# The result's turn runs ahead of the scores in their block, states are turned six steps behind their load, and the opening's pieces get other ranks

## The chip, the cores and the metric

One core of a Trainium2 chip runs the whole program. The metric is the device time of one execution in microseconds (us); of several runs the median is taken. Engines go by the names of the profile: PE is TensorE (matrix products, and transposes as products with an identity), PEld its weight loads, DVE is VectorE, ACT is ScalarE, SP issues the transfers (DMA).

## The reference, cut to what matters

```python
# x: B=8, H=8, S=512, D=64; state: B, H, Ns=32, D
scale = 1 / sqrt(D)
a      = softmax(scale * x @ state.T)          # [B,H,S,Ns]
xread  = a @ state                             # [B,H,S,D]
a2     = softmax(scale * state @ x.T)          # [B,H,Ns,S]
sread  = a2 @ x                                # [B,H,Ns,D]
attn   = concatenate([xread, sread], axis=2)   # [B,H,S+Ns,D]
x2     = attn.transpose(0, 2, 1, 3).reshape(4352, 512)
h      = x2 @ w_in                             # w_in: 512 x 2048
g      = h * clip(h + 3, 0, 6) / 6             # hardswish
out    = g @ w_out                             # w_out: 2048 x 512
```

All inputs and the output are float32.

## The kernel before, in words

**Numbers.** Float32 products at full precision are made of three fast products: each operand is split into a high part (ACT, L246) and a low part (DVE, L247), and hi·hi, hi·lo and lo·hi are added up in one bank (`product`, L831). Only the first batch's first quarter of the hidden width uses plain float32 matmuls (L860 for the first product, L900 for the second), since its split operands are not there yet.

**Steps.** The hidden width of 2048 has 16 pieces of 128. A step is one batch (512 tokens) with one such piece, or one piece for the 256 state tokens at the end; there are 144. `first(n)` (L836) makes h into a bank `ps_h` (L831, or L860); ACT (L881) and DVE (L883) make g of it; L246 and L247 split g; `second(n)` (L890) multiplies with the rows of w_out (L831, or L900) into the four accumulators `acc`. The second product of a step comes two steps behind its first. The order of the steps is: batch 0 quarter 0, batch 1 quarter 0, batch 0 quarter 1, batch 1 quarter 1, then the later quarters of batch 0, those of batch 1, batches 2 to 7 whole, and the state tokens.

**Tokens' side.** The read of the states by tokens is folded into the weights: W' is state times w_in by heads (matmuls L458 in 64x32 tiles of the array), so that the first product is the softmax weights `aT` times W'. The scores of a batch are L458 as well, w_in's place being taken by x turned (`xT`), and `stT` being the state turned. Where W' of batch 0 is made for the first quarter, its columns come in three pieces of 128, 128 and 256; the row with 256 columns is called the second half in what follows.

**State's side.** `scores_by_columns` (L654) is one block on PE: the 16 score matmuls of batch b, then, from batch 2 on, two riders of the batch before: a transpose (L791) of the result of the batch before that one (the tile `tmp` `sr`, which DVE's L805 makes) and the 64 small matmuls of the read (L796), both into one bank `ps_h`. DVE copies the turned result into `sread_t` (L770), the input of the state tokens' steps. `tokens_read_alone` runs the same for the last batch, with no scores.

**States.** `load_state` (L368) lets SP load the state of a batch into `st_raw`, a tile with one buffer (L382 from batch 2 on, 4 transfers of 32x4x32 in a row of the order), and DVE turn it into `stT` (L389). The scores of the batch, and its W', read `stT`.

**Order.** Every piece of work is told to a planner (class `Plan`) with its engine, a cost, a rank, the keys it reads and writes, and pieces that it must stand behind. The planner holds a modelled clock for PE, DVE, ACT and SP; each time it takes, among the pieces that can start nearly first on an engine, the one of lowest rank (the number may be negative), and so fixes a serial order for each of the four. A rank is about the number of the step in which the piece is wanted. Some tiles have few buffers, which the planner holds too: `raw` 3, `ot` 2, `tmp` 10, `ps_h` 2, `ps_s` 2, one each of `xb` and `st_raw`. Up to the first step of the program, planned gaps of PE are filled with transposes of the identity into `ps_h` (L1127), which compute nothing.

**The opening's lines.** x of batch 0 is scored by rows on PE; DVE ends that softmax with L582. L630 turns the softmax weights back (8 transposes). L546 turns x of batch 1, in two halves of 8 transposes, by way of two `ps_s` banks that ACT copies out. L316, L320 and L327 are DVE's passes that clamp and round a weight (into `w_in`, `raw` or `early`); L303 loads weights. L693 and its neighbours are the softmax of batch 0's late scores (L458 out of `xT`), which only the state's side needs, and whose small transposes are L731. L354 is a low part of w_out made from a `raw` tile. L445 loads x turned into `raw` for batch 2, and L752 moves the blocks of the read weights from one `tmp` tile to another, 32 small transfers for batch 1. L674 turns scores on DVE.

**Where ranks stand.** `weights` (L987) has a row for each early piece of w_in and w_out; its last two numbers are the ranks of the passes on DVE and of the load. `LATE` and `LATE_STEP` do the same for the late pieces of w_in, and `HALVES` for a piece split in halves. `fetch` (L1058) tells the loads of a later batch: the state of batch b with step s0, which is 7 steps ahead of the step in which its scores are told.

Of the kernel before, what the change touches and what calls it, by code (L numbers as in the profile page):

```python
# [10 lines left out]
F32 = mybir.dt.float32  # L11
# [138 lines left out]
def tile_state_attention_then_hardswish_ffn(  # L150
# [8 lines left out]
    nc = tc.nc  # L159
# [209 lines left out]
    def load_state(b, rank, after=()):  # L369
        key = ("st_raw", b)  # L370

        def load():
            raw = get(key, lambda: att.tile([P, NG, D], F32, name="st_raw", bufs=1))
            for u in range(NG):
                nc.sync.dma_start(raw[:, u, :], st_v[b, :, :, u, :])

        def load_blocks():
            raw = get(key, lambda: att.tile([P, NG * D], F32, name="st_raw", bufs=1))
            for u in range(NG):
                for k in range(D // NS):  # L380
# [8 lines left out]
        V(0.22, rank + 1.0, lambda: nc.vector.transpose(  # L389
            get(("stT", b), lambda: att.tile([P, P], F32, name="stT")), made[key]), [key], [("stT", b)])  # L390

    def x_key(b):
        return ("ot", "x1") if b == 1 else ("xb", b)
# [258 lines left out]
    def scores_by_columns(b, rank, after=(), name="C"):  # L652

        ps = [("ps_s", (name, b, u)) for u in range(NG)]  # L654
        riders = [tokens_read(b - 1, "ps_h")] if b >= TURNED or name == "L" and b else []

        def run():
            all_heads(b, [bank(k) for k in ps], lambda q: xT(b, q))
            for _, read, _, _, _ in riders:
                read()  # L660

        T(1.22 + sum(r[0] for r in riders), rank, run,
          [("stT", b)] + [xT_key(b, q) for q in range(NQ)] + [k for r in riders for k in r[2]],
          ps + [k for r in riders for k in r[3]], after)
        for r in riders:
            r[4]()
        return ps
# [107 lines left out]
    def tokens_read(b, tag="ps_s"):  # L775
# [11 lines left out]
        last_key = [("tmp", ("sr", c)) for c in last]  # L787

        def read():
            for key in last_key:  # L790
                nc.tensor.transpose(bank(pr)[:, place(1)], tmp(key)[:, : NG * D], ident)  # L791
            for u in range(NG):
                for j in range(J):
                    for q in range(NQ):
# [9 lines left out]
        def then():  # L804
# [3 lines left out]
                [pr, ("r2", (b, 0))], [sr_key])  # L808
            for c in last:
                put(c, pr, place(1))  # L810
        return 1.0 + 0.11 * len(last), read, [*t_key, *x_parts, *last_key], [pr], then

    def tokens_read_alone(b, rank, after=()):
        cost, read, reads, writes, then = tokens_read(b)
        T(cost + 0.2, rank, read, reads, writes, after)
        then()

    def result_turned(b, rank, after=()):
# [156 lines left out]
    for seg, (b, c0, c1) in enumerate(segments):  # L975
# [8 lines left out]
    seen = set()  # L984

    weights = [
        (0, "in", 0, 1, ("early0", 0, 0), -5.67, -19.58), (1, "in", 1, 1, ("early0", 0, 1), -3.50, -8.04),  # L987
        (2, "in", 2, 2, ("early1", 0), 0.77, -7.20), (-0.34, "out", 0, 1, ("raw", ("out", 0)), -2.50, -6.17),
        (-0.90, "out", 1, 1, ("raw", ("out", 1)), -0.36, -1.02), (0.55, "out", 2, 1, ("raw", ("out", 2)), 2.49, -3.00),
        (5.05, "out", 3, 1, ("early3", 0, 0), 2.13, -1.44),  # L990
    ]
# [3 lines left out]
    PLACES = {  # L995
# [68 lines left out]
    at(6, lambda: [f(4.88 + 0.2 * k) for k, f in enumerate(late_halves)])  # L1064
    at(9, halves_of_first, 9.5)
    for b, s0 in (0, 4), (1, 8):

# [24 lines left out]
    load_x(0, -14.96)  # L1092
    weights_until(0.7)
    load_state(1, -4.23)
    accs = [f"acc{q}" for q in range(NQ)]
    take_in(0, -14.82, (), accs)
    tokens_by_rows(0, lambda k: -2.51, lambda k: (), accs)
    load_x(1, -3.76)
    for n in range(len(steps)):
        tell(n)  # L1100
# [6 lines left out]
        elif b < 2 and n % FPC == 0:  # L1107
            ends = wp_parts[b, c][1:] + [FPC]
            for f0, f1 in zip(wp_parts[b, c], ends):
                weights_until(n + f1 - 1)  # L1110
                s = n - 3 + f0
                wprime(b, [(c, f0, f1)], s + 0.41 if n else (11.83, -6.49, 0.01)[f0],
                       ["acc2", "acc3"] if n == 0 and f1 < 3 else None,
                       [first_of[s]] if n >= 8 else ())
        if n == 0:
            take_in(1, -0.41, [scores_at[0]])
            rank1 = lambda k: (1.71, 2.50, 1.58, -2.06, 0.41)[k]
            tokens_by_columns(1, rank1, scores_by_columns(1, 1.99, [wp_at[0, 0, 2]]))
        for f, a in events.get(n, ()):
            f(*a)  # L1120
        first(n)
# [36 lines left out]
```

## Time and profile before

| | us |
|---|---|
| runs of before (3) | 663.09 to 663.54 |
| median | 663.51 |
| the profiled execution | 663.73 |
| its span (first to last instruction) | 661.9 |
| around the span | 1.8 |
| busy: PE, DVE, ACT | 651.0, 420.2, 310.8 |
| PE's three-part second products, L831 into `acc` | 3 x 528 matmuls, 209.1 + 205.6 + 205.9 |
| PE's first products, L831 into `ps_h` with split weights of a batch | 3 x 248, 90.7 + 89.7 + 89.7 |
| scores and W', L458 | 384 matmuls, 24.0 |

Busy times of matmuls overlap, since each is counted from its issue to its modelled end; what one costs in a row of them is the distance between two starts. The page divides the span into 40 slices; the busy share of PE in tenths is 8 in the second slice, 0 in the first, 7 in the last and 9 in all others. The clock that PE was granted is 9 (90% or more) in every slice. The transfers move 46.26 MB in all, and their engines are busy 9, 8, 0 and 7 tenths in the first four slices, and less behind.

How the lines are read: in the timeline and in the list of PE's rows a line has the start in us, the time from its start to the end of its last instruction, the engine, the line of the kernel, the operation, the tile written and the tiles read, then for PE the tile of the array (128*128 is all of it), the shape and the type, and how many instructions it groups; in brackets stands the idle time before it, and the instruction that ended it. In the list of groups the number behind the count is the time busy, then the mean of one in ns, then the idle time before. Tiles of one name are told apart by buffer numbers in the order's rows and not in the trace's.

### The profile page before, as it was taken

Reading aid. Unit: us, or ns where it says so; the run is one execution under the profiler, and the core shown is the slowest. Engines: PE = TensorE matmul, PEld = TensorE weight load, DVE = VectorE, ACT = ScalarE, POOL = GpSimd, SP = SyncE. Lnnn points to the kernel's source line nnn. Section 1 sums busy time; section 2 is a strip of 40 time slices with the busy share of each in tenths; the row PEclk is TensorE's granted clock in tenths of the full one; section 3 lists DMA queues with packets and bytes.
Section 4 is the critical chain, followed back from the end, with each engine's and each line's share of the span. In section 5 each row is a group of like instructions: output and inputs, shape, how many; then the busy total and the mean of one; then the engine's idle time right before and its main releaser. Section 6 shows DMA issues by size and latency. Waiting matters only on the chain.

```text
span 661.9 us, 9937 instructions
## 1 busy us (share of the span) xinstructions
PE 651.0 (98%) x3950; PEld 502.5 (76%) x3950; DVE 420.2 (63%) x697; ACT 310.8 (47%) x520; POOL 1.0 (0%) x7
## 2 busy tenths in 40 slices
PE   8899999999999999999999999999999999999997
PEld 7446777777686877787877877787778788788896
DVE  4998999885846945953677356944585353543542
ACT  5888777543523543443444343633343343333542
POOL 0000000000000000000000000000000000000000
PEclk9999999999999999999999999999999999999999
DMA  9807452415052243314050503132131001000101
GB/s 272 308 0 214 133 181 81 96 27 139 13 109 74 34 70 94 66 26 70 1 132 9 84 5 109 24 52 44 65 65 24 8 1 65 1 0 1 64 0 33
DMA packets 130894, 46.26 MB, mean 70 GB/s; under 512 B 119200, under 2 KB 121248, under 8 KB 130720
## 3 DMA queue, kind: packets, MB, share of 16 engines
q1 hardware_dynamic: 130704, 45.37, 27.9%
q8 instruction: 31, 0.51, 0.3%
q10 hardware_dynamic: 144, 0.26, 0.1%
q14 instruction: 15, 0.12, 0.1%
HBM read 33.03 MB, written 8.91 MB: 63 GB/s over the span
## 4 chain that ended last, share of the span: by engine, by line
PE 92%; DVE 3%; SPq 2%; DMA 2%; issue 0%; ACT 0%; DVEq 0%; ACTq 0%
PE acc L831 53%; PE ps_h L831 28%; PE ps_s L458 4%; PE acc L900 2%; DMA st_raw<-in_state_dram 2%; PE ps_h L458 2%; SPq L752 2%; PE ps_h L796 1%; PE ps_h L860 1%; PE ps_s L611 1%; SPq L382 0%; DVE g L883 0%; PE acc L546 0%; DVE g_lo L247 0%; DVE s L571 0%
## 5 line engine op out<-in xcount | busy, mean ns | idle before, releaser
L831 PE MATMUL acc<-w_out_hi,g_hi 128*128 128x512 f32 x528 | 209.1, 396 | 0.0
L831 PE MATMUL acc<-w_out_hi,g_lo 128*128 128x512 f32 x528 | 205.6, 389 | 0.3 <-DVE g_lo L247 0.3
L831 PE MATMUL acc<-w_out_lo,g_hi 128*128 128x512 f32 x528 | 205.9, 390 | 0.0
L881 ACT ACTIVATE g<-ps_h,three 128x512 f32<-128x512 f32 (+1 forms) x144 | 95.6, 664 | 212.5 <-PE ps_h L831 208.2
L883 DVE SCALAR_TENSOR_TENSOR g<-g,ps_h 128x512 f32<-128x512 f32 (+1 forms) x144 | 94.5, 657 | 136.9 <-ACT g L881 136.2
L831 PEld LDWEIGHTS acc<-w_out_hi,g_hi 128*128 128x128 f32 x528 | 99.1, 188 | 35.5 <-issue 13.4
L246 ACT CAST g_hi<-g 128x512 fp32r<-128x512 f32 (+1 forms) x140 | 83.3, 595 | 85.1 <-DVE g L883 84.8
L247 DVE TENSOR_TENSOR g_lo<-g,g_hi 128x512 fp32r<-128x512 f32 (+1 forms) x140 | 92.0, 657 | 46.2 <-ACT g_hi L246 43.8
L831 PEld LDWEIGHTS acc<-w_out_hi,g_lo 128*128 128x128 f32 x528 | 99.1, 188 | 21.8 <-DVE g_lo L247 0.8
L831 PEld LDWEIGHTS acc<-w_out_lo,g_hi 128*128 128x128 f32 x528 | 99.2, 188 | 18.9
L831 PE MATMUL ps_h<-aT_hi,wp_hi 128*128 128x512 f32 (+1 forms) x248 | 90.7, 366 | 0.0
L831 PE MATMUL ps_h<-aT_hi,wp_lo 128*128 128x512 f32 (+1 forms) x248 | 89.7, 362 | 0.0
L831 PE MATMUL ps_h<-aT_lo,wp_hi 128*128 128x512 f32 (+1 forms) x248 | 89.7, 362 | 0.0
L831 PEld LDWEIGHTS ps_h<-aT_hi,wp_hi 128*128 128x128 f32 x248 | 46.8, 189 | 8.5 <-DVE wp_lo L247 0.3
L831 PEld LDWEIGHTS ps_h<-aT_lo,wp_hi 128*128 128x128 f32 x248 | 46.8, 189 | 8.2 <-DVE early L316 0.3
L831 PEld LDWEIGHTS ps_h<-aT_hi,wp_lo 128*128 128x128 f32 x248 | 46.8, 189 | 7.3
L831 PE MATMUL ps_h<-aT_hi,wp 128*128 128x512 f32 x128 | 44.6, 389 | 0.0
L831 PEld LDWEIGHTS ps_h<-aT_hi,wp 128*128 128x128 f32 x128 | 24.0, 188 | 5.0
L831 PE MATMUL ps_h<-aT_lo,wp 128*128 128x512 f32 x64 | 24.9, 389 | 0.0
L458 PE MATMUL ps_s<-w_in,stT 64*32 64x512 f32 (+1 forms) x384 | 24.0, 557 | 0.0
L537 DVE STREAM_TRANSPOSE tmp<-raw 128x512 f32<-128x512 f32 x24 | 16.4, 699 | 6.5 <-DMA raw<-in_x_dram 6.5
L247 DVE TENSOR_TENSOR wp_lo<-ps_s,wp_hi 128x512 fp32r<-128x512 f32 (+1 forms) x34 | 19.8, 621 | 0.3 <-ACT wp_hi L246 0.3
(119 smaller groups left out, 506.4 us busy)
## 6 DMA issues: line engine op xcount, KB each, us to landing
out_dram<-ot SPq DMA_DIRECT2D x8, 1024.0 KB, 4.5
early<-in_moe_w_in_dram SPq DMA_DIRECT2D x7, 1024.0 KB, 7.1
xb<-in_x_dram SPq DMA_DIRECT2D x28, 256.0 KB, 4.1
raw<-in_x_dram SPq DMA_DIRECT2D x96, 64.0 KB, 2.1
early<-in_moe_w_out_dram SPq DMA_DIRECT2D x4, 1024.0 KB, 5.5
raw<-in_moe_w_out_dram SPq DMA_DIRECT2D x7, 512.0 KB, 4.4
raw<-raw SPq DMA_DIRECT2D x96, 32.0 KB, 2.0
early<-in_moe_w_in_dram SPq DMA_DIRECT2D x2, 512.0 KB, 5.3
```

The lines of the kernel that those rows point to most:

```text
L246: S_(cost, rank, lambda: nc.scalar.copy(hi(), src()), reads, [writes[0]])
L247: V(cost, rank, lambda: nc.vector.tensor_tensor(lo(), src(), hi().bitcast(F32), op=ALU.subtract), [*reads, writes[0]], [writes[1]])
L458: nc.tensor.matmul(out[u][cols, :], made["stT", b][rows, cols], moving(q)[rows], start=True, stop=True,)
L537: V(0.7, rank, lambda q=q, key=key: nc.vector.transpose(xT(b, q), made[key][:, q % 2]), [(*key, q % 2, u, k) for u in range(2) for k in ra ...
L611: nc.tensor.matmul(out[:, j, q], xT(b, q)[:, js], apart[:, q], start=True, stop=True,)
L752: nc.sync.dma_start(dst[:, :, q], src[:, :, c])
L796: nc.tensor.matmul(bank(pr)[cols, u * D : (u + 1) * D], e2T(b, u)[:, j * P + q * NS : j * P + (q + 1) * NS], x_tile(b, True)[:, NG * q + u ...
L831: nc.tensor.matmul(ps, l, r, start=start and k == 0, stop=stop and k == n - 1)
L860: nc.tensor.matmul(bank(ps), made["wp_32", (b, k)][:, g, fs], a_first(g), start=g == 0, stop=g == NG - 1)
L881: S_(cost + 0.05, rank, lambda: nc.scalar.activation(g(), bank(ps)[:, :width], AF.Relu, bias=three), [ps], [g_key])
L883: V(cost, rank, lambda: nc.vector.scalar_tensor_tensor(g(), g(), 6.0, bank(ps)[:, :width], op0=ALU.min, op1=ALU.mult), [ps], [g_key])
L900: nc.tensor.matmul(bank(acc), made["g_hi", n][:, js], plain_out[i][1](), start=opens, stop=closes)
```

## The change

There are three edits.

The transposing of a result on PE is taken out of `read` in `tokens_read` and handed back as a function of its own, `first`, which `scores_by_columns` calls ahead of the scores; `tokens_read_alone` calls it directly ahead of the read, as it did.

DVE's turn of a state is taken out of `load_state`. A new function, `turn_state`, tells it, six steps behind the load, with a rank that is five higher than the one it had.

Ranks of the opening's pieces of weights, x, W' and softmax are replaced by others.

```diff
@@ load_state
         plan.add("Q", 1.8, rank, load_blocks, (), [key], after, 400.0)
-        V(0.22, rank + 1.0, lambda: nc.vector.transpose(
-            get(("stT", b), lambda: att.tile([P, P], F32, name="stT")), made[key]), [key], [("stT", b)])
+
+    def turn_state(b, rank, after):
+
+        key = ("st_raw", b)
+        V(0.22, rank, lambda: nc.vector.transpose(
+            get(("stT", b), lambda: att.tile([P, P], F32, name="stT")), made[key]), [key], [("stT", b)], after)
@@ scores_by_columns
         def run():
+            for r in riders:
+                r[5]()
             all_heads(b, [bank(k) for k in ps], lambda q: xT(b, q))
-            for _, read, _, _, _ in riders:
-                read()
+            for r in riders:
+                r[1]()
@@ tokens_read
         def read():
-            for key in last_key:
-                nc.tensor.transpose(bank(pr)[:, place(1)], tmp(key)[:, : NG * D], ident)
             for u in range(NG):
...
-        return 1.0 + 0.11 * len(last), read, [*t_key, *x_parts, *last_key], [pr], then
+
+        def first():
+            for key in last_key:
+                nc.tensor.transpose(bank(pr)[:, place(1)], tmp(key)[:, : NG * D], ident)
+        return 1.0 + 0.11 * len(last), read, [*t_key, *x_parts, *last_key], [pr], then, first
@@ weights and ranks
-        (0, "in", 0, 1, ("early0", 0, 0), -5.67, -19.58), (1, "in", 1, 1, ("early0", 0, 1), -3.50, -8.04),
...
+        (0, "in", 0, 1, ("early0", 0, 0), -22.54, -44.86), (1, "in", 1, 1, ("early0", 0, 1), -24.76, -19.99),
...
-    LATE, LATE_STEP, HALVES = (2.35, 6.00), (0.38, 0.50), 1.45
+    LATE, LATE_STEP, HALVES = (28.48, 9.19), (-14.22, -0.40), -9.26
@@ fetch
         at(s0 + 1, lambda: load_state(b, s0, [first_of[s0]]))
+        at(s0 + 7, lambda: turn_state(b, s0 + 6, [first_of[s0 + 6]]))
```

What the ranks do is read from the order. **PE, the opening**: the rows from the end of batch 1's first half of turned x to the first L900 of batch 0 (`acc`). `ident,ot` are turns of x, `ident,tmp` turns of softmax weights, `w_in,stT` pieces of W', `xT,stT` batch 0's late scores, `w_in,wp` the plain first product. Before:

```order
L1127 MATMUL ps_h<-ident 128x128 x5
L630 MATMUL acc_316<-ident,tmp 128x128 x4
L630 MATMUL acc_324<-ident,tmp 128x128 x4
L546 MATMUL ps_s<-ident,ot 128x128 x8
L860 MATMUL ps_h<-w_in_322,wp_243 128x512 x4
L458 MATMUL ps_s<-w_in_187,stT 32x256 x8
L900 MATMUL acc_382<-raw,g 128x512
```

After:

```order
L1140 MATMUL ps_h<-ident 128x128 x2
L550 MATMUL ps_s<-ident,ot 128x128 x8
L634 MATMUL acc_326<-ident,tmp 128x128 x4
L634 MATMUL acc_332<-ident,tmp 128x128 x4
L462 MATMUL ps_s<-xT,stT 32x512 x8
L872 MATMUL ps_h<-w_in_338,wp_243 128x512 x4
L737 MATMUL ps_s<-ident,tmp 128x128 x8
L912 MATMUL acc_394<-raw,g 128x512
L912 MATMUL acc_399<-raw,g 128x512
L912 MATMUL acc_404<-raw,g 128x512
L462 MATMUL ps_s<-w_in_160,stT 32x256 x8
```

Three of five fillers are gone; the second half of the turns stands ahead of the softmax weights' turns; batch 0's late scores stand ahead of the first product and their small transposes (L737 in the new lines, L731 before) behind it; the piece of W' with 256 columns stands behind three second products instead of ahead of the first. (A plain float32 matmul of the order is two instructions of the trace: x4 of `w_in,wp` here is x8 there, x8 of `xT,stT` is x16. Transposes count once.) Some 340 rows later, from step 28 on, PE's order is the old one but for the second edit.

**DVE, the opening**: from the end of the first softmax (L582 before, L586 after) to the w_in row that the piece with 256 columns reads (`w_in_187` before, `w_in_160` after). Before:

```order
L582 TENSOR_TENSOR tmp<-tmp,s_263 128x512 x2
L320 SCALAR_TENSOR_TENSOR raw<-raw 128x512
L327 SCALAR_TENSOR_TENSOR raw<-raw 128x512
L316 TENSOR_SCALAR early_106<-early_106 128x1024
L320 SCALAR_TENSOR_TENSOR early_106<-early_106 128x1024
L327 SCALAR_TENSOR_TENSOR w_in_187<-early_106 128x4x256
```

After:

```order
L316 TENSOR_SCALAR early_106<-early_106 128x1024
L699 TENSOR_REDUCE nm_354<-ps_s 128x1
L701 TENSOR_SCALAR nm_354<-nm_354 128x1
L699 TENSOR_REDUCE nm_362<-ps_s 128x1
L701 TENSOR_SCALAR nm_362<-nm_362 128x1
L316 TENSOR_SCALAR raw<-raw 128x512
L320 SCALAR_TENSOR_TENSOR raw<-raw 128x512
L706 TENSOR_SCALAR r_365<-r_365 128x2
L708 RECIPROCAL r_365<-r_365 128x2
L895 SCALAR_TENSOR_TENSOR g<-g,ps_h 128x512
L327 SCALAR_TENSOR_TENSOR raw<-raw 128x512
L320 SCALAR_TENSOR_TENSOR early_106<-early_106 128x1024
L327 SCALAR_TENSOR_TENSOR w_in_160<-early_106 128x4x256
```

The three rows ahead of those of after are the old ones. Between the clamp of `early` and its rounding now stand the softmax of batch 0's late scores (L699 to L708), three passes over `raw` and the first g (L895).

**PE, a block of scores** (here that of batch 3's scores, with the read of batch 2 and batch 1's result): the rows from the last first product to the next second product. Before:

```order
L831 MATMUL ps_h<-aT_hi,wp_lo 128x512
L458 MATMUL ps_s<-tmp,stT 32x512 x8
L791 MATMUL ps_h<-ident,tmp 128x128
L796 MATMUL ps_h<-xb,raw 32x64 x32
L831 MATMUL acc_1859<-w_out_hi_718,g_hi 128x512
```

After:

```order
L843 MATMUL ps_h<-aT_hi,wp_lo 128x512
L818 MATMUL ps_h<-ident,tmp 128x128
L462 MATMUL ps_s<-tmp,stT 32x512 x8
L800 MATMUL ps_h<-xb,raw 32x64 x32
L843 MATMUL acc_1856<-w_out_hi_738,g_hi 128x512
```

The transpose has changed places with the scores; the rest of the block stands as it did. This is so in six blocks.

**DVE, a state's turn** (that of batch 3, during step 28; `st_raw` has one buffer, and L674 turns the scores of batch 2 whose softmax follows). Before:

```order
L805 TENSOR_TENSOR tmp<-ps_h,r_752 128x128
L770 COPY sread_t<-ps_h 128x128
L674 STREAM_TRANSPOSE tmp<-ps_s 128x512 x2
L389 STREAM_TRANSPOSE stT<-st_raw 128x128
L247 TENSOR_TENSOR g_lo<-g,g_hi 128x512
L565 TENSOR_REDUCE m_1597<-tmp 128x16
```

After:

```order
L247 TENSOR_TENSOR wp_lo<-ps_h,wp_hi 128x512 x2
L247 TENSOR_TENSOR wp<-ps_s,wp 128x512 x2
L247 TENSOR_TENSOR aT_lo<-tmp,aT_hi 128x512
L764 STREAM_TRANSPOSE raw<-tmp 128x512
L895 SCALAR_TENSOR_TENSOR g<-g,ps_h 128x512
L764 STREAM_TRANSPOSE raw<-tmp 128x512
L895 SCALAR_TENSOR_TENSOR g<-g,ps_h 128x512
L247 TENSOR_TENSOR g_lo<-g,g_hi 128x512 x2
L393 STREAM_TRANSPOSE stT<-st_raw 128x128
```

The turn stands some 30 rows later, behind the softmax of batch 2 and not ahead of it. On SP the four loads of that state now stand ahead of the store of an output tile (`out_dram<-ot`, 128x2048) and not behind it.

More of the change, by code (lines that the diff above doesn't have):

```diff
@@ L810, in then, with run @@
                 put(c, pr, place(1))
-        return 1.0 + 0.11 * len(last), read, [*t_key, *x_parts, *last_key], [pr], then
+        def first():
+            for key in last_key:
+                nc.tensor.transpose(bank(pr)[:, place(1)], tmp(key)[:, : NG * D], ident)
+        return 1.0 + 0.11 * len(last), read, [*t_key, *x_parts, *last_key], [pr], then, first
     def tokens_read_alone(b, rank, after=()):
-        cost, read, reads, writes, then = tokens_read(b)
-        T(cost + 0.2, rank, read, reads, writes, after)
+        cost, read, reads, writes, then, turn_last = tokens_read(b)
+        def run():
+            turn_last()
+            read()
+        T(cost + 0.2, rank, run, reads, writes, after)
         then()
@@ L986, in tile_state_attention_then_hardswish_ffn @@
     weights = [
[L987 to L990 removed]
+        (0, "in", 0, 1, ("early0", 0, 0), -22.54, -44.86), (1, "in", 1, 1, ("early0", 0, 1), -24.76, -19.99),
+        (2, "in", 2, 2, ("early1", 0), 6.93, -9.11), (-12.37, "out", 0, 1, ("raw", ("out", 0)), -6.07, -6.01),
+        (-19.24, "out", 1, 1, ("raw", ("out", 1)), 1.25, 3.51), (-3.21, "out", 2, 1, ("raw", ("out", 2)), 0.76, 2.18),
+        (-1.73, "out", 3, 1, ("early3", 0, 0), 3.93, 1.24),
     ]
@@ L1111, in tile_state_attention_then_hardswish_ffn @@
                 s = n - 3 + f0
-                wprime(b, [(c, f0, f1)], s + 0.41 if n else (11.83, -6.49, 0.01)[f0],
+                wprime(b, [(c, f0, f1)], s + -0.92 if n else (39.35, -26.67, -5.60)[f0],
                        ["acc2", "acc3"] if n == 0 and f1 < 3 else None,
```

16 lines of the change are left out of this document (8 added, 8 removed).

## The prediction

> **What bounds the kernel now.** I read the page's busy line and the chain that ended last first, then the timeline of TensorE (PE) for every pause, then who ended each pause.
>
> ```profile
> span 661.9 us, 9937 instructions
> PE 651.0 (98%) x3950; PEld 502.5 (76%) x3950; DVE 420.2 (63%) x697; ACT 310.8 (47%) x520; POOL 1.0 (0%) x7
> PE 92%; DVE 3%; SPq 2%; DMA 2%; issue 0%; ACT 0%; DVEq 0%; ACTq 0%
> 20.28:29.00 8.72, 6.87 (x48) 3.78 (x46) 8.48 (x14) 7.59 (x17) 0.00 (x0) 1.00 0.99 369
> 29.00:111.30 82.30, 82.30 (x501) 53.23 (x502) 77.28 (x120) 64.55 (x100) 0.00 (x0) 1.00 0.43 134
> ```
>
> PE makes 92% of the chain. So the change can only gain in three places: where PE waits, where PE runs filler, and where it pays for changing shape. The last two rows are stretches (length, then PE, weight load, DVE, ACT). From 29.00 to 111.30 us PE has no pause, but DVE is busy 77.28 of 82.30 us: a second limit lies close behind. I look at the three places in turn.
>
> **1. The opening.**
>
> ```profile
> 20.28 0.71 PE L1127 MATMUL ps_h<-ident 128*128 128x128 f32 x5
> 21.55 1.26 PE L630 MATMUL acc<-ident,tmp 128*128 128x128 f32 x8 [0.56 <-DVE tmp L582]
> 22.64 1.04 PE L546 MATMUL ps_s<-ident,ot 128*128 128x128 f32 x8
> 23.51 3.60 PE L860 MATMUL ps_h<-w_in,wp 128*128 128x512 f32 x8
> 27.04 0.66 PE L458 MATMUL ps_s<-w_in,stT 64*32 64x256 f32 x16
> 29.00 1.17 PE L900 MATMUL acc<-raw,g 128*128 128x512 f32 x2 [1.29 <-DVE g L883]
> 36.94 1.09 PE L458 MATMUL ps_s<-xT,stT 64*32 64x512 f32 x16
> 37.96 1.98 PE L860 MATMUL ps_h<-w_in,wp 128*128 128x512 f32 x4
> ```
>
> Dead time of PE before: 0.71 of filler (L1127) and 0.56 of waiting before L630, 1.29 before the first L900; 2.56 us in all. After 29.00 PE runs through.
>
> By the changed order, the second half of batch 1's turns (L546 x8) and batch 0's scores (the L458 of 36.94, which holds PE 1.02 us, 36.94 to 37.96, and about 0.09 to enter) stand ahead of the first L860. I walk it with the rows' durations. The turns run from about 20.7 to 21.65, held by ScalarE's copies out of the two ps_s banks. L630 follows to 22.6, the scores to 23.7. The first L860 needs ScalarE's copies of L630, which now stand behind the two copies of the turns and end near 23.55, where they ended 23.49 before. So L860 starts at 23.7 instead of 23.51, with 1.11 us of scores already done. Its eight instructions end at 27.2, the state weights' turns (eight at 0.11) at 28.05. There the wait for the first g (1.29 before) should be over: VectorE's g now ends near 28.0.
>
> What is late next is the second half of batch 0's first W' (the L458 of 27.04), since its w_in columns come later on VectorE:
>
> ```profile
> 20.80 1.29 DVE L582 TENSOR_TENSOR tmp<-tmp,s 128x512 f32<-128x512 f32 x2
> 23.34 0.69 DVE L316 TENSOR_SCALAR early<-early 128x1024 f32<-128x1024 f32 x1
> 25.33 1.23 DVE L327 SCALAR_TENSOR_TENSOR w_in<-early 128x1024 uint32<-128x1024 uint32 x1
> 27.65 0.69 DVE L327 SCALAR_TENSOR_TENSOR raw<-raw 128x512 uint32<-128x512 uint32 x1
> L693 DVE TENSOR_REDUCE nm<-ps_s 128x1 f32<-128x512 f32 x16 | 10.9, 683 | 0.0
> ```
>
> From the end of L582 (22.1) VectorE's new order has up to that w_in row: four 512-wide passes over raw at about 0.69 and one clamp at 0.42, one clamp at 0.69, two L693 at 0.68, a g at 0.66, two 1024-wide passes at 1.23, and four tiny rows (0.6 together): 9.0 us, so 31.1, where it was 26.56. PE, after six L900 instructions at 0.45, comes there at 30.8. Dead time after: about 0.6 ahead of L860 and 0.3 here, 0.9 in place of 2.56, a gain of 1.6.
>
> I do not take all of it. Walking on, VectorE stays about 1 us ahead at batch 1's first product (aT_lo 46.9, PE 47.9), 0.7 ahead at the first g_lo (55.1, 55.8), and level with PE at the second W' piece of w_in1 (both near 67.7). One or two pauses of 0.1 to 0.3 us are likely. And a second queue follows:
>
> ```profile
> 120.41 0.68 DVE L354 TENSOR_TENSOR w_out_lo<-raw,w_out_hi 128x512 fp32r<-128x512 f32 x1
> 121.12 8.30 SPq L445 DMA_DIRECT2D raw<-in_x_dram  x16
> 130.08 22.14 SPq L752 DMA_DIRECT2D tmp<-tmp  x32
> 153.29 1.27 PE L796 MATMUL ps_h<-xb,tmp 128*32 128x64 f32 x64
> ```
>
> SP issues without a break from 121.12, when L354 frees raw, to 152.2, the end of the 32 L752. The last of these are read by the second half of L796, near 153.9; a landing takes about 2 us. PE cannot come much earlier to L796 than SP does, and L354 moves by some 1.0 us in my walk. I take **1.3 us** for the opening. Its ends: 2.56 (no dead time left), and a loss of 1.0 (VectorE a little late at each of those three places; 0.3 apiece).
>
> **2. The result's turn ahead of the scores.** It happens six times (L791 into ps_h, 150 to 480 us); at 551 us the turn stands alone, with no scores.
>
> ```profile
> 262.90 0.39 PE L831 MATMUL ps_h<-aT_hi,wp_lo 128*128 128x512 f32 x1
> 263.22 1.09 PE L458 MATMUL ps_s<-tmp,stT 64*32 64x512 f32 x16
> 264.24 0.33 PE L791 MATMUL ps_h<-ident,tmp 128*128 128x128 f32 x1
> 264.50 1.10 PE L796 MATMUL ps_h<-xb,raw 128*32 128x64 f32 x64
> 265.53 0.50 PE L831 MATMUL acc<-w_out_hi,g_hi 128*128 128x512 f32 x1
> 550.96 0.39 PE L831 MATMUL ps_h<-aT_hi,wp_lo 128*128 128x512 f32 x1
> 551.19 0.27 PE L791 MATMUL ps_s<-ident,tmp 128*128 128x128 f32 x1
> 551.39 1.10 PE L796 MATMUL ps_s<-xb,raw 128*32 128x64 f32 x64
> ```
>
> Read the starts. Before: L831 to L458 0.32, L458 to L791 1.02, L791 to L796 0.26, L796 to L831 1.03; 2.63 us. At 550.96 the turn stands directly behind an L831 and the pair costs 0.23 and 0.20. So after: 0.23 (L831 to turn), 0.20 (turn to scores, taken as turn to L796 there), 1.02 (the scores, as 36.94 to 37.96, whatever follows) and 1.03; 2.48. The gain is 0.15 us a time, **0.9 us** for six. The cover needed: the ps_h bank must be free 1.3 us sooner. Its last reader, the g two products back, has long ended: in the trace that is over 2 us before, and over 0.8 us at the tightest (b=3). If it weren't, the price is PE's wait for it. Ends: 0 and 1.5.
>
> The Trainium skill's page TensorEngine Tiling (Array Packing), section Tiling Modes, says that a change of tiling mode drains the engine. By it the block goes from four changes to three; the page gives no price. If all four cost the same, a quarter of what the rows show beyond plain spacing would go: 0.09 at 262.90, 0.51 behind the scores, 0.15 behind the turn, 0.25 at and behind 265.53; 1.0, so 0.25 a time and 1.5 us for six. By the rows the change behind the scores stays, and 0.9 is what goes.
>
> **3. States turned later.**
>
> ```profile
> 155.04 1.30 DVE L674 STREAM_TRANSPOSE tmp<-ps_s 128x512 f32<-128x512 f32 x2
> 159.19 0.31 DVE L389 STREAM_TRANSPOSE stT<-st_raw 128x128 f32<-128x128 f32 x1 [2.85 <-DMA st_raw<-in_state_dram]
> 166.00 0.69 DVE L247 TENSOR_TENSOR g_lo<-g,g_hi 128x512 fp32r<-128x512 f32 x1
> 165.28 0.39 PE L831 MATMUL acc<-w_out_hi,g_lo 128*128 128x512 f32 x1
> 165.68 0.50 PE L831 MATMUL acc<-w_out_hi,g_hi 128*128 128x512 f32 x1
> 166.01 0.40 PE L831 MATMUL acc<-w_out_lo,g_hi 128*128 128x512 f32 x1
> 166.74 0.50 PE L831 MATMUL acc<-w_out_hi,g_lo 128*128 128x512 f32 x1 [0.33 <-DVE g_lo L247]
> 167.07 0.39 PE L831 MATMUL acc<-w_out_hi,g_hi 128*128 128x512 f32 x1
> ```
>
> VectorE stands 2.85 us at batch 3's state, and the whole softmax of batch 2 behind it. That reaches PE at 165.28: the five starts to 167.07 are 1.79 us apart where four spacings of 0.227 make 0.91, so 0.88 is lost. In the new order the turn stands some 35 rows later, and SP issues the four state loads ahead of the 1 MB output store instead of behind it. VectorE's g_lo comes 2.85 us sooner against a lateness of 0.88, so all of it goes, with about 0.1 for a late weight load at 172.6 I round to **0.95 us**. The other state turns wait for nothing in the list of waits (one wait, 2.8 us), and no scores come sooner than the turn's new place: gain 0. The output store comes 3 us later, which nobody on PE waits for. Ends: 0 and 1.0.
>
> **Sum.** 1.3 + 0.9 + 0.95 = 3.15 us. The profiled execution took 663.73 us, its span 661.9 and 1.8 around it; 660.58 follows. The median of the runs is 663.51, 0.22 lower; I predict **660.4 us**. A measurement of this kernel can tell about 0.2% (1.3 us) from no change, so "faster" is below 662.2.
>
> **Rivals.**
> - *The opening gains nothing* (25%): VectorE's 94% between 29 and 111 us, or SP's run to 152.2, takes it all back. For it: the level slack near 67.7 and the run of 54 issues. Against: PE's 501 instructions there never wait now, and VectorE waits too now. Places 2 and 3 stay: 663.5 - 1.85 = 661.6.
> - *The opening gains all* (13%): no new wait. 663.5 - 2.56 - 1.85 = 659.1.
> - *The state's turn moves, PE's wait stays* (8%), because g_lo at 166 hangs on something else (ScalarE's exponentials of the same block). The rows 159.19 to 166.00 on VectorE without an idle stretch speak against. 661.3.
> - *Changes of shape cost alike*, the rule above (4%): 1.5 for place 2, 659.8.
> - *Slower* (4%): VectorE's queue ahead of batch 1's first product, now one serial run with the state softmax drawn into it. It decides from the point where aT_lo comes over 0.9 us late; each us beyond is one us on PE. To lose all of 3.15 it must come 4.1 us late; at 5.6 us late, 665.0. Two exponentials on ScalarE ahead of the first g are the place where such lateness would start.
> - The forecast keeps 46%, between 659.7 and 661.1.
>
> Faster by over 0.2%: forecast, the full opening, the equal price, most of the first and third rival: 0.86. Within 0.2%: their tails, 0.10. Slower: 0.04. The range reaches to the full opening below and to the first rival with a little of place 2 or 3 missing above: 659.0 to 662.3.
>
> **What the changed profile would show.** First L860 near 23.7 with the xT scores ahead of it; L900 near 28.1; a pause of about 0.3 us at the next L458. PE's rows of batch 0's last W' (w_in3, 108.79 now) some 1.5 us sooner; L796 of 153.29 about 1.2 sooner, its duration telling whether SP's run held it. Six blocks of 2.48 us from the last L831 to the next. No wait of VectorE on st_raw, and no pause over 0.1 us on PE between 155 and 175. It would be wrong if VectorE's g_lo or W' rows end PE's pauses between 30 and 110 us, or if the turn waits for ps_h.

## The result, and the profile after

The changed kernel took 659.49 us (median of 5 runs, 658.89 to 661.03) against 663.51 us (5 runs, 663.06 to 666.52) before: 4.02 us less, a ratio of 0.9935 with a 95% interval of 0.9914 to 0.9955. The forecast was 660.4, with 659.0 to 662.3 around it. The profiled execution took 660.14 us, 3.59 less than that of before.

The page of the changed kernel: busy time, and the chain that ended last. Then two stretches of the span (length; busy time of PE, weight load, VectorE, ScalarE, GpSimd; clock).

```profile
span 658.4 us, 9928 instructions
PE 649.1 (99%) x3947; PEld 502.6 (76%) x3947; DVE 419.6 (64%) x697; ACT 311.0 (47%) x520; POOL 1.0 (0%) x7
PE 96%; DMA 3%; ACT 1%; SPq 0%; issue 0%
20.00:29.00 9.00, 8.98 (x60) 5.38 (x58) 8.60 (x20) 7.91 (x18) 0.00 (x0) 1.00 1.00 376
29.00:111.30 82.30, 82.14 (x497) 53.02 (x496) 78.62 (x117) 66.46 (x101) 0.00 (x0) 1.00 0.44 136
```

VectorE is gone from the chain (3% before), PE has 96% of it, and the opening's PE is full. (The page of before has PE at 8 tenths in the first slice, as in the second, and not at 0 as was said above.) To see where the time went I set the same PE instruction of both traces side by side; the difference of their starts can only change where one kernel loses or saves time. A first product a little behind the place from which both orders are the same starts at 111.99 us before and 111.03 after: 0.96 sooner. Just ahead of batch 2's scores it is still 0.96, behind that block 1.13, behind batch 2's W' 2.86, at the end 3.60. So in this pair of executions the opening gave 0.96, the stretch around 165 us 1.73, and the six blocks 0.90.

**The opening.** PE's timeline after (start, length, engine, line, and so on as before; L529 is L525 of before, L550 L546, L634 L630, L462 L458, L872 L860, L912 L900, L843 L831):

```profile
19.38 0.30 PE L529 MATMUL ps_s<-ident,st_raw 128*128 128x128 f32 x1 [0.99 <-DMA st_raw<-in_state_dram]
20.72 0.38 PE L1140 MATMUL ps_h<-ident 128*128 128x128 f32 x2
21.12 1.14 PE L550 MATMUL ps_s<-ident,ot 128*128 128x128 f32 x8
22.10 1.15 PE L634 MATMUL acc<-ident,tmp 128*128 128x128 f32 x8
23.18 1.09 PE L462 MATMUL ps_s<-xT,stT 64*32 64x512 f32 x16
24.20 3.70 PE L872 MATMUL ps_h<-w_in,wp 128*128 128x512 f32 x8
27.73 1.04 PE L737 MATMUL ps_s<-ident,tmp 128*128 128x128 f32 x8
28.61 2.87 PE L912 MATMUL acc<-raw,g 128*128 128x512 f32 x6
31.40 0.66 PE L462 MATMUL ps_s<-w_in,stT 64*32 64x256 f32 x16
```

The turn of batch 1's state (L529) waits for its load and starts at 19.38; before, its counterpart started at 18.94. Counted from there the opening gained 1.40 us, not 0.96. The 1.29 ahead of the first second product (L912) is gone: L737's eight turns fill it, and the g (VectorE's L895, 27.53 to 28.22) is there when they end. But 35 us later PE waits at W', in its weight loads, for ScalarE's L703, the exponentials of batch 1's late scores, which still read the `ps_s` banks. ScalarE's queue shows why:

```profile
65.18 0.14 PEld L462 LDWEIGHTS ps_s<-w_in,stT 64*32 64x32 f32 x2 [0.54 <-ACT tmp L703]
65.85 0.18 PEld L462 LDWEIGHTS ps_s<-w_in,stT 64*32 64x32 f32 x14 [0.53 <-ACT tmp L703]
62.72 1.23 ACT L308 ACTIVATE early<-early,eighth 128x1024 uint32<-128x1024 uint32 x1 [1.63 <-DMA early<-in_moe_w_out_dram]
64.36 0.68 ACT L703 ACTIVATE tmp<-ps_s,nm 128x512 f32<-128x512 f32 x1
```

L308 stands ahead of the exponentials and sat 1.63 us until its piece of w_out had landed. Starts of PE around it show about 0.85 us lost. The order before has no such wait.

**A block of scores** (the turn is L818 now, the reads L800):

```profile
259.88 0.39 PE L843 MATMUL ps_h<-aT_hi,wp_lo 128*128 128x512 f32 x1
260.11 0.27 PE L818 MATMUL ps_h<-ident,tmp 128*128 128x128 f32 x1
260.31 1.09 PE L462 MATMUL ps_s<-tmp,stT 64*32 64x512 f32 x16
261.33 1.10 PE L800 MATMUL ps_h<-xb,raw 128*32 128x64 f32 x64
262.36 0.50 PE L843 MATMUL acc<-w_out_hi,g_hi 128*128 128x512 f32 x1
```

0.23, 0.20, 1.02, 1.03: 2.48 us where the block took 2.63. Five of the six are 0.15 shorter, batch 2's 0.17 (2.80 before, 2.63 after).

**The stretch near 165 us.** After, VectorE goes straight from the turned scores (L680, 153.90 to 155.18) to g_lo, and PE has no pause. Before, there was a second one, which my five starts did not reach. PE's rows of before again, and the weight loads of before:

```profile
167.86 1.09 PE L458 MATMUL ps_s<-w_in,stT 64*32 64x512 f32 x16
168.74 1.75 PE L458 MATMUL ps_h<-w_in,stT 64*32 64x512 f32 x16
170.43 0.50 PE L831 MATMUL acc<-w_out_hi,g_hi 128*128 128x512 f32 x1
169.41 0.18 PEld L458 LDWEIGHTS ps_h<-w_in,stT 64*32 64x32 f32 x14 [0.56 <-DVE g L883]
```

and the same place after:

```profile
165.83 1.09 PE L462 MATMUL ps_s<-w_in,stT 64*32 64x512 f32 x16
166.71 1.06 PE L462 MATMUL ps_h<-w_in,stT 64*32 64x512 f32 x16
167.70 0.50 PE L843 MATMUL acc<-w_out_hi,g_hi 128*128 128x512 f32 x1
```

A group of 16 lasts 1.06 us when nothing stops it; the one of 168.74 lasted 1.75. Its weights waited for the `ps_h` bank, which a g (L883) late on VectorE still read. The same 2.85 us of VectorE's wait reached PE twice: 0.88 at g_lo, 0.69 here, and some 0.13 at a weight load behind it that waited for VectorE's wp_lo (172.60).

### The profile page after: what moved, and what is told of

The parts are those of the page before. It is cut to its first block, busy times and chain, and to the rows that moved or that the text cites. A ratio compares the mean times of both kernels' runs of the same rounds, so it can differ in the third digit from the quotient of the medians.

```text
span 658.4 us, 9928 instructions
## 1 busy us (share of the span) xinstructions
PE 649.1 (99%) x3947; PEld 502.6 (76%) x3947; DVE 419.6 (64%) x697; ACT 311.0 (47%) x520; POOL 1.0 (0%) x7
## 4 chain that ended last, share of the span: by engine, by line
PE 96%; DMA 3%; ACT 1%; SPq 0%; issue 0%
PE acc L843 54%; PE ps_h L843 29%; PE ps_s L462 4%; PE acc L912 2%; PE ps_h L462 2%; DMA st_raw<-in_state_dram 1%; DMA early<-in_moe_w_out_dram 1%; PE ps_h L872 1%; PE ps_h L800 1%; PE ps_s L615 1%; PE ps_s L550 0%; PE acc L550 0%; PE ps_h L1140 0%; ACT tmp L703 0%; ACT early L308 0%; SPq L375 0%
## 5 line engine op out<-in xcount | busy, mean ns | idle before, releaser
L843 PE MATMUL acc<-w_out_hi,g_hi 128*128 128x512 f32 x528 | 208.8, 396 | 0.0
L843 PE MATMUL acc<-w_out_lo,g_hi 128*128 128x512 f32 x528 | 205.9, 390 | 0.0
L843 PE MATMUL acc<-w_out_hi,g_lo 128*128 128x512 f32 x528 | 205.6, 389 | 0.0
L895 DVE SCALAR_TENSOR_TENSOR g<-g,ps_h 128x512 f32<-128x512 f32 (+1 forms) x144 | 94.7, 657 | 137.9 <-ACT g L893 136.6
L843 PEld LDWEIGHTS acc<-w_out_hi,g_hi 128*128 128x128 f32 x528 | 99.1, 188 | 34.7 <-issue 12.1
L843 PEld LDWEIGHTS acc<-w_out_hi,g_lo 128*128 128x128 f32 x528 | 99.1, 188 | 21.0
L843 PEld LDWEIGHTS acc<-w_out_lo,g_hi 128*128 128x128 f32 x528 | 99.2, 188 | 19.1
L843 PE MATMUL ps_h<-aT_hi,wp_hi 128*128 128x512 f32 (+1 forms) x248 | 90.3, 364 | 0.0
L843 PE MATMUL ps_h<-aT_hi,wp_lo 128*128 128x512 f32 (+1 forms) x248 | 89.8, 362 | 0.0
L843 PE MATMUL ps_h<-aT_lo,wp_hi 128*128 128x512 f32 (+1 forms) x248 | 89.7, 362 | 0.0
L843 PEld LDWEIGHTS ps_h<-aT_hi,wp_hi 128*128 128x128 f32 x248 | 46.8, 189 | 8.6 <-ACT w_out_hi L352 0.4
L843 PEld LDWEIGHTS ps_h<-aT_lo,wp_hi 128*128 128x128 f32 x248 | 46.8, 189 | 8.0 <-issue 0.3
L843 PEld LDWEIGHTS ps_h<-aT_hi,wp_lo 128*128 128x128 f32 x248 | 46.8, 189 | 7.2
L843 PE MATMUL ps_h<-aT_hi,wp 128*128 128x512 f32 x128 | 44.6, 389 | 0.0
L843 PEld LDWEIGHTS ps_h<-aT_hi,wp 128*128 128x128 f32 x128 | 24.0, 188 | 5.0
L843 PE MATMUL ps_h<-aT_lo,wp 128*128 128x512 f32 x64 | 24.9, 389 | 0.0
L462 PE MATMUL ps_s<-w_in,stT 64*32 64x512 f32 (+1 forms) x384 | 24.6, 557 | 0.2
```

Of the source, the lines that this page charges most:

```text
L462: nc.tensor.matmul(out[u][cols, :], made["stT", b][rows, cols], moving(q)[rows], start=True, stop=True,)
L843: nc.tensor.matmul(ps, l, r, start=start and k == 0, stop=stop and k == n - 1)
L895: V(cost, rank, lambda: nc.vector.scalar_tensor_tensor(g(), g(), 6.0, bank(ps)[:, :width], op0=ALU.min, op1=ALU.mult), [ps], [g_key])
```

## The experiments

Line numbers differ by a few between these kernels. "Place" means the start of the same PE instruction against the profile of before.

**One edit each, and the changed kernel once more.** `turn_only` has the new functions `first` and the two loops in `scores_by_columns`, `state_only` has `turn_state` and its line in `fetch`, `ranks_only` has all the new numbers and nothing else.

> The kernel before, with the result's turn ahead of the scores and nothing else of the change. The six blocks of the changed kernel each came 0.15 us sooner at their end than before. Theory (place counts, not only the number of shape changes): 6 x 0.15 = 0.9 us, 662.6 against 663.5. Rival (all shape changes cost alike): 1.5 us, 662.0. Rival (the turn now waits for its ps_h bank): PE shows a wait of the turn, and the gain is under 0.5 us. The pauses of PE between 165 and 170 us stay as before in every theory.

> The kernel before, with the state turned six steps behind its load and nothing else; SP's order is that of before, the output store ahead of the state's loads. Theory A (VectorE's place decides): VectorE no longer waits for st_raw near 156, and both pauses of PE go, that at g_lo (0.88) and that of the second half of W' that waited for VectorE's g (0.70), with 0.14 of late weight loads: 1.7 us, 661.8. Rival B (the recorded forecast's sum, only the pause at g_lo): 0.95 us, 662.6. Rival C (the loads ahead of the store were what helped): VectorE waits at the new place, gain under 0.3 us.

> The kernel before, with the new ranks and neither of the other two edits. The new ranks also put batch 3's state loads ahead of the output store on SP. Theory A (two ways to the same end): the state lands near 155, VectorE's turn at its old place hardly waits, and this kernel has the opening's gain, 1.4 us counted from where batch 1's state has landed, and the 1.7 us near 165 as well: 3.1 us, 660.4. Rival B (VectorE's place is needed): VectorE still waits near 155, the opening's gain alone, 662.1. Rival C (the opening gains nothing by itself): 663.5 less what comes of the state.

> The changed kernel once more. The changed kernel's runs lie 2.1 us apart, those of before 0.5. Theory A (early transfers): in the changed kernel's profile the first loads of w_in landed 0.8 us later than in that of before and batch 1's state 0.44 us later on PE, with the same order of transfers up to there; so another profile should show another start and the same distances behind it, and a median between 659.0 and 660.2. Rival B (the start is later because of the new ranks): batch 1's state is turned on PE near 19.4 us again, as in the other profile, and not near 18.9. In both, the pause of PE of 0.85 us near 65 us (a bank of W' that ScalarE's exponentials still read) comes back.

| | median us (runs) | ratio, 95% |
|---|---|---|
| before, same chip | 663.48 (27) | |
| turn_only | 663.24 (11) | 0.9991, 0.9981 to 1.0 |
| state_only | 661.99 (11) | 0.9978, 0.9969 to 0.9987 |
| ranks_only | 662.88 (11) | 0.9991, 0.9982 to 1.0 |
| all_again | 659.90 (5) | 0.9945, 0.9933 to 0.9958 |

The three alone gain 0.24, 1.49 and 0.60, together 2.33; the change gains 3.58 here. The traces say why.

*turn_only*: at each of the six blocks the place moves by 0.15, 0.9 in all, as expected. The profile as a whole is no faster (663.76): a load of x for batch 1 landed late (PE's L546 waited 0.72 for it at 20.68), and the whole program ran 0.67 behind from there. Of the first block's 0.15, 0.09 went again near 166 us, where VectorE's stall at batch 3's state still stood, and 0.13 near 200 us at a weight load that waited for g_lo, VectorE having stood 1.31 us for a load of x. So the mechanism is shown by the trace; the median's interval runs from no change to 1.26 us and holds both 0.9 and nothing.

*state_only*: the place is 0.01 sooner just ahead of 165 us, 1.73 sooner behind 173, and 1.76 sooner from the next block to the end: theory A, to 0.06. On SP the loads still stand behind the output store:

```profile
151.75 0.54 SPq L939 DMA_DIRECT2D out_dram<-ot  x1
152.33 2.99 SPq L382 DMA_DIRECT2D st_raw<-in_state_dram  x4
```

So VectorE's place alone was enough.

*ranks_only*: a miss. The opening's gain is there, 1.41 at 111.99 us, as theory A had it. But 0.9 of it goes again, since the new ranks move VectorE's turn too, and the wrong way: ahead of the g of step 27 and of the scores' turn. VectorE and PE of that kernel:

```profile
156.45 0.31 DVE L389 STREAM_TRANSPOSE stT<-st_raw 128x128 f32<-128x128 f32 x1 [6.98 <-DMA st_raw<-in_state_dram]
156.69 0.65 DVE L883 SCALAR_TENSOR_TENSOR g<-g,ps_h 128x512 f32<-128x512 f32 x1
157.39 0.50 PE L831 MATMUL ps_h<-aT_hi,wp_hi 128*128 128x512 f32 x1 [1.18 <-DVE g L883]
151.33 2.01 SPq L382 DMA_DIRECT2D st_raw<-in_state_dram  x4
```

The loads do stand ahead of the store and are issued by 153.3; it did not help, because VectorE had already been waiting since 149.5 and held the g that PE's next `ps_h` bank needs. With these ranks the state edit is worth more than alone: without it the stretch costs 0.9 more than before, with it 1.7 less.

*all_again*: the spread that this run was to explain is not the changed kernel's alone: the five runs of before lie 3.5 us apart, by one of 666.52. Batch 1's state was turned at 19.08; in twelve profiles, three with the old ranks and nine with the new, the turn begins between 18.78 and 19.38, the first profile of the change being the latest. Theory A holds: it is the early transfers' chance. The wait near 65 us, which both theories had at 0.85, shrank to 0.13: the piece of w_out had landed by 61.70 there, and by 62.72 in the first profile of the change. The opening gave 1.98 in this profile, counted at 111.99, and the state's stretch 1.73 again.

**The order in the block, and one state.** In `turn_behind` and `reads_first` only the loops of `run` change places; `one_state` keeps the later turn for batch 3.

```diff
 # turn_behind                                # reads_first
+all_heads(...)                               +for r in riders: r[5]()
+for r in riders: r[1]()                      +for r in riders: r[1]()
+for r in riders: r[5]()                      +all_heads(...)
 # one_state, in fetch
+if b == 3:
+    at(s0 + 7, lambda: turn_state(b, s0 + 6, [first_of[s0 + 6]]))
+else:
+    at(s0 + 1, lambda: turn_state(b, s0 + 1.0, ()))
```

> The changed kernel with the result's turn behind the reads, so next to full-size products again but at the block's end. Theory A (one change of tile shape less is what pays, wherever the turn stands next to full-size products): the block takes 2.48 us from the last first product to the next second product, as in the changed kernel, and the time is that of the changed kernel within 0.3 us. Rival B (standing ahead is what pays, the turn's 0.11 and its changes of shape hide behind the product in front): 2.6 us a block, the changed kernel's time plus 0.7 to 0.9.

> The changed kernel with the order turn, reads, scores in the block (the scores last). As many changes of shape as in the changed kernel. Theory A (a price by the instruction in front: 0.52 us behind 512-wide scores whatever follows, 0.15 behind 64-wide reads): the step from the last read to the first score is 0.15 us, the block stays at 2.48 within 0.1. Rival B (every change costs the same): no difference either, but then the step from reads to scores and the step behind the scores have the same excess. Rival C (the scores, now 1 us later, reach VectorE too late): PE waits for g_lo some 10 us behind a block, and the time is worse by more than 0.5 us.

> The changed kernel with the state of batch 3 alone turned six steps behind its load; the other five are turned one rank behind their load as in the kernel before. Theory A (one stall, at batch 3, was all that the later turns removed): the time of the changed kernel within 0.3 us, and no wait of VectorE for st_raw over 0.3 us. Rival B (the other five give something too): 0.3 us or more slower than the changed kernel.

They took 659.27, 660.18 and 659.35 us in this order (4 runs each; 663.70 before). A block with the turn behind the reads, then one with the reads first:

```profile
205.89 0.39 PE L843 MATMUL ps_h<-aT_hi,wp_lo 128*128 128x512 f32 x1
206.21 1.09 PE L462 MATMUL ps_s<-tmp,stT 64*32 64x512 f32 x16
207.23 1.10 PE L800 MATMUL ps_h<-xb,raw 128*32 128x64 f32 x64
208.26 0.33 PE L818 MATMUL ps_h<-ident,tmp 128*128 128x128 f32 x1
208.35 0.48 PE L843 MATMUL acc<-w_out_hi,g_hi 128*128 128x512 f32 x1
```

```profile
207.06 0.39 PE L843 MATMUL ps_h<-aT_hi,wp_lo 128*128 128x512 f32 x1
207.29 0.27 PE L818 MATMUL ps_h<-ident,tmp 128*128 128x128 f32 x1
207.49 1.10 PE L800 MATMUL ps_h<-xb,raw 128*32 128x64 f32 x64
208.52 1.09 PE L462 MATMUL ps_s<-tmp,stT 64*32 64x512 f32 x16
209.54 0.50 PE L843 MATMUL acc<-w_out_hi,g_hi 128*128 128x512 f32 x1
```

2.46 and 2.48, as in the change. So "ahead" is not what pays; what pays is that the turn stands next to full-size products, at either end. In `reads_first` too the scores hold PE 1.02 us, and the step from the last read to the next group takes 0.15, whatever follows.

But most of the scores' 0.52 (the step from the last of them to what follows) is not the price of a change. Sixteen matmuls of the same tile and width hold PE 0.88 us where sixteen more of their kind stand behind them (165.83 to 166.71 in the rows of W' above), so the change behind the scores costs 0.14, 1.02 less 0.88. The reads start in fours, with 0.04 from one four to the next; the change behind them costs 0.11, 0.15 less 0.04. So theory A's two prices, 0.52 and 0.15, do not stand. Rival B, that every change costs about the same, fits these rows as well, and since both gave 2.48 the time cannot separate them. Of rival C nothing shows: PE does not wait for g_lo behind the blocks.

The six blocks are not quite alike. At batch 2's block, near 150 us, `reads_first` took 4.29 us, 1.66 more than the change, which theory A's 2.48 missed and which makes it the slowest of the three. Its reads show the cause:

```profile
150.13 0.75 PE L800 MATMUL ps_h<-xb,tmp 128*32 128x64 f32 x34
151.16 0.27 PE L800 MATMUL ps_h<-xb,tmp 128*32 128x64 f32 x2 [0.29 <-DMA tmp<-tmp]
151.81 0.27 PE L800 MATMUL ps_h<-xb,tmp 128*32 128x64 f32 x2 [0.37 <-DMA tmp<-tmp]
152.44 0.61 PE L800 MATMUL ps_h<-xb,tmp 128*32 128x64 f32 x26 [0.36 <-DMA tmp<-tmp]
```

Each pair of reads waits for one more of the 32 block moves. That is SP's long run, as a limit that PE now meets.

*one_state* is as fast as the change, and no wait of VectorE for `st_raw` is in its list: theory A, one stall was all.

**The two limits that the opening meets.** `exp_sooner` changes one rank of the changed kernel; `act_moves` lets ScalarE issue 4 of the 32 moves; `three_more` has both, and the turn behind the reads.

```diff
-    LATE, LATE_STEP, HALVES = (28.48, 9.19), (-14.22, -0.40), -9.26
+    LATE, LATE_STEP, HALVES = (28.48, 8.2), (-14.22, -0.40), -9.26
 # act_moves, in weights_moved
+on_act = g == 1 and c == 3
+(nc.scalar if on_act else nc.sync).dma_start(dst[:, :, q], src[:, :, c])
```

> The changed kernel with one rank changed (the late scores of batch 1: 9.19 to 8.2), so that ScalarE runs the two exponentials of batch 1's late scores ahead of a g_hi instead of behind it; PE's order is the same. In two of three profiles with the new ranks PE waited 0.65 to 0.85 us near 65 us for the banks that these exponentials read; they stood behind a pass over a late w_out piece that landed at 62.3 to 62.7 us, and where it landed at 61.7 there was no wait. Theory A: with the exponentials 0.5 us earlier the wait is under 0.3 us even where the piece lands late, and the median is 0 to 0.6 us under the changed kernel's. Rival B (the reads of SP's long run near 152 us hold PE anyway): the wait near 65 goes, a pause inside the reads of 152 us grows by as much, and the time stays.

> The changed kernel with four of the 32 block moves of batch 1 (0.67 us of SP each) issued by ScalarE instead of SP; the order is otherwise the same. In the profiles PE paused inside the reads near 152 us by 0.15 to 0.58 us, the longer the earlier PE came, and in the kernel with the reads first by 1.8. Theory A (SP's run of issues holds the reads): without four of them the pause is 0, the block near 152 takes 2.48 us like the others, and the median is 0.2 to 0.6 us under the changed kernel's. Rival B (the last moves' transfers, not their issue, are late): the pause stays. Rival C (a wait of ScalarE for the blocks holds its exponentials or g): PE has a new pause between 128 and 140 us.

> The changed kernel with all three: four moves issued by ScalarE, batch 1's exponentials earlier, the result's turn behind the reads. If the gains add up: 0.2 to 0.6 for SP's run, 0 to 0.6 for the exponentials (which SP's run no longer takes back), 0.2 to 0.3 for the turn behind the reads (0.05 in each of six blocks, counted to the second second product): 658.3 to 659.0. Rival (each finds another limit): within 0.2 us of the changed kernel.

They took 659.66, 659.04 and 658.81 us (5 runs each), ratios 0.9939 (0.9925 to 0.9953), 0.9927 (0.9915 to 0.994) and 0.9926 (0.9912 to 0.9939). The reads near 152 us of `exp_sooner`, and those of `three_more` (L805):

```profile
150.82 0.79 PE L800 MATMUL ps_h<-xb,tmp 128*32 128x64 f32 x38
151.89 0.61 PE L800 MATMUL ps_h<-xb,tmp 128*32 128x64 f32 x26 [0.28 <-DMA tmp<-tmp]
152.43 0.50 PE L843 MATMUL acc<-w_out_hi,g_hi 128*128 128x512 f32 x1
```

```profile
150.94 1.25 PE L805 MATMUL ps_h<-xb,tmp 128*32 128x64 f32 x64
152.12 0.33 PE L823 MATMUL ps_h<-ident,tmp 128*128 128x128 f32 x1
152.20 0.48 PE L848 MATMUL acc<-w_out_hi,g_hi 128*128 128x512 f32 x1
```

PE reaches the reads at nearly the same time. With 32 moves on SP they last 1.61 to the next product; with 28 they last 1.18 to the turn, the 1.17 of the undisturbed ones (152.18 to 153.35 in the first profile of the change). So the issue of the moves was the limit, and 0.44 its price there. The Trainium skill, "DMA: Bandwidth & Descriptors", section Rules for kernel authors, says that spreading transfers over issuing engines only saves the issuing engine's time; that is what was saved here. Theory A's other number missed: batch 2's block took 2.63 us in `act_moves`, as in the change, and not 2.48; its reads take 1.17 where those of other batches take 1.03, for a reason that no run shows. Rival C did not come: ScalarE spent 2.87 us on the four issues, and PE's place moved by 0.03 us between 112 and 151 us.

`exp_sooner` itself did not decide its question: the wait near 65 us was gone, but in its profile the piece of w_out had landed by 61.29, and `one_state`, without the new rank, had none either with a landing by 61.14. `act_moves` with the old rank had about 1.0 us of it. `turn_behind` (old rank) and `three_more` (new rank) do decide it, with landings by 61.78 and 61.83. The W' near 65 us in the one, then in the other:

```profile
64.39 1.21 PE L462 MATMUL ps_s<-w_in,stT 64*32 64x256 f32 x16
64.54 0.66 PE L462 MATMUL ps_s<-w_in,stT 64*32 64x256 f32 x16
```

The old rank waits about 0.55 us, the new one not at all: the mechanism of theory A is shown, its gain in time is not. The medians do not tell these kernels from the change: their intervals overlap. `three_more` has the lowest median of all, 658.81; that it beats the change is not shown.

## Why the prediction was right, and where its terms were off

**The opening (1.3).** Counted from the turn of batch 1's state the pair of profiles gives 1.40, and `ranks_only` alone 1.38. Without that correction, at 111.99 us, it lies between 0.96 and 2.31 in nine profiles with the new ranks, and at 2.12 or more in the three that have no wait near 65 us. What the two medians of the change leave for it, 4.02 and 3.58 less 0.90 and 1.73, is 1.39 and 0.95 (an estimate). So 1.3 is the right size, but that one pair hit it to 0.1 is luck. The walk held: less the 0.44 of the late state, the first plain product is at 23.76 (23.7 forecast) and the first second product at 28.17 (28.1). Wrong were the places of the waits behind: none at the W' of 31.40, where I had 0.3 (VectorE's row for it ended at 31.22), and not VectorE but ScalarE behind a late transfer near 65 us, up to 1.0 where I had 0.1 to 0.3. SP's run (49 issues to 152.2, not 54) did hold PE as feared, by 0.27 to 0.44 in four profiles whose opening had gained 1.87 to 2.31, by 0.14 in `ranks_only`, and not in that of the change.

**The turn (0.9).** Right to the hundredth: the walk gave 2.48 for the block and 2.48 was measured, in all blocks but batch 2's own 2.63. What the forecast had wrong is a price beside it: the 0.51 behind the scores is mostly their own spacing, as shown above, and the change there costs 0.14. So of the rival that all changes of shape cost alike only the number falls, 0.25 a block. With 0.14 in place of 0.51 the four changes of the old block add up to about 0.6, and a quarter of that is 0.15, the forecast's own gain; no run here separates the two. The Trainium skill's page TensorEngine Tiling (Array Packing), section Tiling Modes, says only that a change drains; the trace agrees that each costs something, from 0.09 behind a product to 0.15 behind the turn in the old block.

**States (0.95).** The step that failed as to size is the one that read the loss from "the five starts to 167.07", and from it the end of 1.0. The lateness of VectorE reached PE a second time 1.7 us on, inside the next W', through a bank and not through g_lo. Measured: 1.73 in the pair, 1.75 in `state_only`. I had taken the rows of W' for undisturbed because no idle stood on their own line; their length, 1.75 against 1.09 of the group in front, told it. The rest of the step also credits SP's new order; `state_only` shows that it wasn't needed and `ranks_only` that it wasn't enough.

**The sum.** 3.15 forecast; with 1.73 in place of 0.95 it is 3.93, and 4.02 was measured between the medians. The same kernel gave 3.58 the second time, so agreement to 0.1 us is luck. Two rivals named numbers nearer to 659.49 than the forecast's 660.4, *changes of shape cost alike* 659.8 and *the opening gains all* 659.1, but neither by its mechanism: the blocks gained 0.15 each and not 0.25, and the opening met a new wait.

**The rivals on VectorE.** Its busy share from 29 to 111 us rose from 77.28 to 78.62 of 82.30 us, and it ended no pause of PE there.

## What to carry to other kernels

When an engine off the path waits, follow its lateness through everything that it owes: the tile that the bounding engine reads next, and the buffers that it has yet to give back; each can stop it anew. Compare the length of each group of instructions with a sister group: a pause that lies in the weight loads showed here only as a longer matmul row, with no idle time before it. And before a long step between two groups is called the price of what follows, see how long the step is where more of the same follows.

An instruction that waits for a transfer is best put behind everything on its queue that others wait for. A reordering that frees the bounding engine also moves such instructions: the same ranks gained 1.4 us in the opening and lost 0.9 of it at a turn that had slid forward.

## What the hardware showed that I had not expected

The early transfers differ from one execution to the next, in the same order of issue: the second and third pieces of w_in landed 0.8 us apart between the profiles of before and after, batch 1's state was turned up to 0.6 us apart in twelve profiles, and the late w_out piece near 62 us decided between no wait of PE and one of 1.0. The same kernel's opening came out at 0.96 in one profile and 1.98 in another, so one pair of profiles tells its worth to about 1 us, no better.

What a change of tile shape cost, beyond the step that stands there when the same shape goes on: behind 512-wide scores 0.14 us, behind 64-wide reads 0.11, behind a transpose or a full-size product 0.09 (0.15 behind the turn of the old block), and nothing from the transpose back to a full-size product. The first full-size product behind such a group then takes 0.34 us to the next, not 0.23 (0.31 behind the transpose).
